# Single placing of transfers with new issue costs, a second staging place for the last weight combinations, and a section moved ahead of the first pair

## The chip, the core and the metric

The kernel runs on one core of a Trainium2 chip. The metric is device time in microseconds (us) of one execution. TensorE (PE) multiplies matrices, VectorE (DVE), ScalarE (ACT) and GpSimd (POOL) do elementwise work, and SyncE (SP) issues every transfer of this kernel, in one queue (SPq in the views). Each engine executes its instructions in the order in which the program was written out; between engines, semaphores make an instruction wait.

## The reference

Windowed attention (8 batches, 8 heads, 576 positions, head size 64, window 64), then a feed-forward layer with a squared ReLU over all 4608 tokens:

```python
scores = scale * np.matmul(q, k.transpose(0, 1, 3, 2))
mask = (rel >= 0) & (rel < 64)              # rel = query position - key position
attn = softmax(np.where(mask, scores, -1e9))
x = (attn @ v).transpose(0, 2, 1, 3).reshape(4608, 512)
out = np.maximum(x @ w_in, 0.0) ** 2 @ w_out      # w_in 512 x 2048, w_out 2048 x 512, 64-bit floats
```

## The kernel before

**Tiles.** The 4608 tokens are 12 tiles of 384. The attention of one tile is three sections (section i belongs to tile i // 3). A section has scores on TensorE (S, L233), copying and masking (o, s), a negative row maximum (z, y), exponentials on ScalarE (e, f, L261), sums and reciprocals, a product on POOL (m, L270), transposes on TensorE (X, L274), their masked copy `pt` (x, L278), the values on TensorE (V, L296) and the copies of the result into the tile's x (H, Q; L311, L313). `burst(i, j)` puts the scores of section i and the values of section j on TensorE one behind the other; `cross(i)` puts the transposes.

**Inputs of sections.** `load_qk(b, g)` loads a pair of heads of q and k into one of two halves of `raw`, by 8 transfers (L146); a transpose on VectorE (`turn`, L165) brings it into place. `load_v(b, t)` loads 128 positions of v, by 4 transfers (2 for the last t), L155; a batch's v comes in three parts of 8, 4 and 6 transfers, placed behind the softmax of three sections.

**Feed-forward.** Every matrix is held as a high and a low part, and three products make one. Tiles 0 to 3 are plain: for each of the 16 blocks f of the hidden layer, a first product (12 matmuls, `mm1`, L402), ReLU on ScalarE (`evac`, L411), square on VectorE (L416), the split (L419, L421), and a second product two steps later (9 matmuls, `mm2`, L444). Tiles 4 to 11 go in four pairs by a scheme of seven products in place of eight: `operands(j)` makes sums and differences of the pair's x and splits them (L848, L859, L860), `product(s, n)` is one of the seven products of step s (six matmuls, L896), its results are added up on VectorE (L910) and squared, and `second` (L977, L985) multiplies with w_out. A pair has eight steps s.

**Weight combinations.** The seven products need, beside blocks of w_in itself, sums of blocks. They are made once, during tiles 2 and 3, by `mixing(h)` for h = 0 to 15: six POOL operations (L530, L534) into a scratch `scr`, a cast on ScalarE (C, L536) and a subtraction on VectorE (E, L538) into `mx`, and a store of 512 KB to `mixed` in HBM (F, L540). Scratch and `mx` lie in one of two staging places, the two halves of `wide` (tile `a` in the trace); h below 12 alternates between them, and 12 to 15 all take place 0. The halves of `wide` hold the x of tiles 5 and 6 afterwards, which section 15 and section 18 begin to write. In the same time `keep` stores the split weights to `kept` (L517, 1 MB each). `wi_fetch` (L716, 256 KB) and `wo_fetch` (L724, 512 KB) bring blocks back from `mixed` and `kept` into 13 and 8 slots.

**Order.** Tiles 0 and 1 and the first two steps of tile 2 are written out by hand in a string. Everything behind is listed as operations of a `Plan` with an engine, a cost in us, what each reads and writes, and `lands`, the latency behind it. `in_order` keeps the order of TensorE as listed and simulates the other engines: each takes, of the operations that are ready, the one with the earliest due time (`late`, worked back from TensorE's times). What comes out is a fixed order for each engine. `HOP` (0.12) is added between operations and `SPARE` (1.5) before an operation of SP that waits for an engine other than TensorE. `freed(name)` lets an operation wait until the weight block whose memory the named slab will take has been read for the last time; `SLOTS` says which block that is.

In the pairs, `marks` says at which place a section's bursts and crosses stand: key 2s is ahead of the products of step s, key 2s + 1 is behind them. Section 19 (the second section of tile 6) has key 2: scores of 19 and values of 18 ahead of step 1, its transposes behind step 1.

Of the kernel before, what the change touches and what calls it, by code (L numbers as in the profile page):

```python
# [15 lines left out]
P = 128  # L16
# [13 lines left out]
def window_attention_relu2_ffn(ctx: ExitStack, tc: tile.TileContext, q, k, v, w_in, w_out, out):  # L30
# [108 lines left out]
    def load_qk(b, g):  # L139
        raw = raws[b, g] = raw_t[:, g % 2]  # L140
        for hd in range(2):
            for e in range(2):
                r = slice(32 * (2 * hd + e), 32 * (2 * hd + e) + 32)
                for n, x in enumerate((q, k)):
                    y = x[b, 4 * (g % 2) + 2 * (g // 2) + hd].rearrange("(t i) (e l) -> e i t l", i=32, e=2)[e]
                    sp.dma_start(raw[r, n].rearrange("i (t l) -> i t l", l=32), y)  # L146
# [3 lines left out]
    def load_v(b, t):  # L150
        vt = vts[b, t] = vt_t[:, t]
        for n in range(min(2, NB - 2 * t)):
            s0 = (2 * t + n) * QB
            for m in range(2):
                sp.dma_start(vt[m * QB:(m + 1) * QB, n],  # L155
                             v[b, m * H // 2:(m + 1) * H // 2, s0:s0 + QB, :].rearrange("h s d -> s h d"))
# [363 lines left out]
    def mix(op, h, which=None):  # L520
        p, kk = divmod(h, 2)
        flat = wide()[:, h % 2 if h < LAST_ODD else 0].rearrange("p a b c -> p (a b c)")
# [55 lines left out]
    for g in range(2):  # L578
# [3 lines left out]
    SLOTS = dict(t=0, xb0=1, xb1=2, xb2=3, wi0=4, wi1=5, part0=6, part1=7, hi=8, lo=9, gb0=10, gb1=11,  # L582
                 wo0=12, wo1=13, wo2=14, wo3=15)
# [51 lines left out]
    class Plan:  # L635
# [3 lines left out]
        def __call__(self, engine, cost, do, reads=(), writes=(), lands=0.0, after=()):  # L639
# [10 lines left out]
            self.ops.append((engine, cost, do, before - {n, None}, lands))  # L650

        def in_order(self):
# [10 lines left out]
            for n in reversed(range(len(ops))):  # L663
                if ops[n][0] != "pe":
                    late[n] = min([late[m] for m in after[n]], default=clock) - ops[n][1] - ops[n][4] - HOP
# [8 lines left out]
            out, at_pe = [], 0  # L674
            while len(out) < len(ops):
# [12 lines left out]
                engine, cost, _, _, lands = ops[n]  # L688
                ready[engine].remove(n)
                at_pe += engine == "pe"  # L690
                free[engine] = start + cost
                out.append(n)
                for m in after[n]:
                    missing[m] -= 1
                    hop = SPARE if ops[m][0] == "sp" and engine != "pe" else HOP
                    soon[m] = max(soon[m], start + cost + lands + hop)
# [14 lines left out]
    def wi_fetch(name, source, keys=()):  # L711
# [4 lines left out]
        plan("sp", 0.1, lambda: sp.dma_start(wi_slot(slot).bitcast(F32), source), keys, [("wi", slot)], 4.5,  # L716
             freed(wi_home(slot)[0]) if n < NWI else [])

    def wo_fetch(name, f, tick):
# [4 lines left out]
        plan("sp", 0.1, lambda: sp.dma_start(wo_slot(slot).bitcast(F32), kept[f, :, 1]), tick, [("wo", slot)], 6.0,  # L724
             freed(f"wo{slot // 2}") if n < NWO else [])
# [17 lines left out]
    def values(i):  # L743
        if SPT * 3 <= i < SPT * NTILE:
            plan("pe", 0.95, by(section, "V", i), ["pt"] + [("vt", t) for t in range(5)], ["v_ps0", "v_ps1"])

    def weigh(i):
# [65 lines left out]
    def plain2(n):  # L813
# [3 lines left out]
        for tb in range(NTB) if ends else [None]:  # L817
# [5 lines left out]
            if ends:  # L823
                to = ("part", tb) if t == 3 else ("x", tb)
                plan("act", 0.62, by(put, "Z", t, tb), [("bank", tb + 1)], [to], 0, freed("part0") if t == 3 else [])
                plan("sp", 0.1, by(put, "W", t, tb), [to], [], 3.0)
# [13 lines left out]
    def operands(j):  # L840
# [104 lines left out]
    def second(k, x):  # L945
# [40 lines left out]
        if group == 3:  # L986
            row = (NPLAIN + 2 * j) * TT + tb * P
            plan("sp", 0.1, lambda: sp.dma_start(out[row:row + P, :], parts(tb)), [kp], [], 3.0)
# [6 lines left out]
    for h in range(NMIX, 2 * NP):  # L995
        mixing(h)
    for n in range(2 * NF + LAG, NPLAIN * NF):
# [4 lines left out]
        plain2(n - LAG)  # L1002
        plain_g(n)
# [68 lines left out]
```

## Time and profile before

| | before |
|---|---|
| median of 3 runs | 860.4 us (858.29 to 1754.12) |
| the profiled execution | 860.38 us, span of its instructions 858.5 us |
| TensorE busy | 832.6 us, 97% of the span |
| VectorE, ScalarE, POOL busy | 593.2, 408.7, 185.2 us |
| chain that ended last | TensorE 88%, DMA 5%, SP's queue 4% |
| packets of the transfers | 273,011, of them 190,496 under 512 B |

The profile is one execution on the chip. All times in the views count from the start of the span. Matmuls overlap, so a stretch of TensorE is best read from the start of one group to the start of the next.

### The profile page before, as it was taken

To read this page: it belongs to the slowest core of one execution; us is meant where nothing else is said; L and a number is where in the kernel's file an instruction comes from. 1 tells how busy PE (TensorE), PEld (TensorE's weight loads), DVE (VectorE), ACT (ScalarE), POOL (GpSimd) and SP (SyncE) were. 2 spreads that over 40 slices of the span, in tenths; PEclk is the share of its full clock that TensorE was granted. 3 is DMA by queue.
4 is the path that set the end of the run, shared out by engine and by line. 5 is a ranking of instruction groups with operands and counts; after the bars stand their busy time and mean duration, and the time that the engine had idled before them with its cause. 6 is when DMAs were issued, how large, how long until landed. Compare 5 with 4: busy or idle time off the path is not lost.

```text
span 858.5 us, 17703 instructions
## 1 busy us (share of the span) xinstructions
PE 832.6 (97%) x6754; PEld 763.1 (89%) x6754; DVE 593.2 (69%) x889; ACT 408.7 (48%) x1127; POOL 185.2 (22%) x239
## 2 busy tenths in 40 slices
PE   6799999999988999999999999999999999999998
PEld 5688999899977999899999999999999999999997
DVE  5899995747764766767678766688765668545553
ACT  5787874646444644554453455344355424223221
POOL 1210003207854300112131112131111231111010
PEclk9999999999998999999999999999999999999999
DMA  9989947475786783988997788979874755776421
GB/s 221 226 260 345 338 193 139 83 169 161 184 214 218 166 161 67 288 256 182 204 282 239 212 173 205 279 173 278 254 238 129 228 185 151 264 244 212 134 76 73
DMA packets 273011, 173.92 MB, mean 203 GB/s; under 512 B 190496, under 2 KB 239648, under 8 KB 270880
## 3 DMA queue, kind: packets, MB, share of 16 engines
q1 hardware_dynamic: 272928, 172.80, 72.8%
q8 instruction: 53, 0.87, 0.4%
q14 instruction: 30, 0.25, 0.1%
HBM read 138.15 MB, written 34.60 MB: 201 GB/s over the span
## 4 chain that ended last, share of the span: by engine, by line
PE 88%; DMA 5%; SPq 4%; ACT 2%; DVE 1%; issue 1%; POOL 0%; ACTq 0%; POOLq 0%; DVEq 0%
PE banks L977 29%; PE banks L896 25%; PE banks L402 13%; PE banks L444 13%; PE banks L296 3%; PE banks L233 3%; DMA mixed<-a 2%; PE banks L274 1%; SPq L155 1%; SPq L183 1%; DMA vt<-in_v_dram 1%; ACT sel L261 1%; DMA w<-in_k_dram 1%; DMA w<-kept 1%; SPq L146 1%
## 5 line engine op out<-in xcount | busy, mean ns | idle before, releaser
L977 PE MATMUL banks<-w 128*128 128x512 f32 x1152 | 257.5, 380 | 0.0
L977 PEld LDWEIGHTS banks<-w 128*128 128x128 f32 x1152 | 215.7, 189 | 28.4
L402 PE MATMUL banks<-x,w 128*128 128x384 f32 x768 | 139.4, 332 | 8.6 <-ACT r L411 8.2
L402 PEld LDWEIGHTS banks<-x,w 128*128 128x128 f32 x768 | 128.2, 191 | 14.0 <-ACT r L411 11.3
L444 PE MATMUL banks<-w,g 128*128 128x512 f32 x576 | 136.2, 382 | 0.0
L896 PE MATMUL banks<-x,w 128*128 128x384 f32 x768 | 130.0, 326 | 0.0
L922 POOL TENSOR_TENSOR g<-g 128x384 f32<-128x384 f32 x64 | 59.5, 934 | 319.3 <-ACT g L933 282.6
L896 PEld LDWEIGHTS banks<-x,w 128*128 128x128 f32 x768 | 125.6, 189 | 0.0
L444 PEld LDWEIGHTS banks<-w,g 128*128 128x128 f32 x576 | 106.3, 189 | 14.3 <-DVE g L421 1.1
L261 ACT ACTIVATE sel<-sel,nm 128x64 f32<-128x64 f32 x272 | 90.8, 336 | 21.3 <-DVE nm L255 18.4
L896 PE MATMUL banks<-w 128*128 128x384 f32 x576 | 100.7, 329 | 0.0
L985 DVE TENSOR_TENSOR w<-w,banks 128x512 f32<-128x512 f32 x72 | 49.4, 687 | 69.9 <-PE banks L977 69.9
L896 PEld LDWEIGHTS banks<-w 128*128 128x128 f32 x576 | 93.8, 189 | 2.0
L967 ACT CAST w<-w 128x512 fp32r<-128x512 f32 x48 | 29.8, 620 | 72.9 <-PE banks L977 72.9
L411 ACT ACTIVATE r<-banks 128x384 f32<-128x384 f32 x64 | 31.5, 492 | 59.6 <-PE banks L402 59.1
L270 POOL TENSOR_TENSOR sel<-sel,nm 128x512 f32<-128x512 f32 x33 | 36.4, 1104 | 106.9 <-ACT g L933 57.9
L967 ACT CAST w<-g 128x512 fp32r<-128x512 f32 x48 | 29.6, 620 | 62.3 <-PE banks L977 58.3
L530 POOL TENSOR_TENSOR a<-w 128x256 f32<-128x256 f32 x32 | 25.9, 822 | 121.5 <-DVE w L132 79.5
L261 ACT ACTIVATION_READ_ACCUMULATOR sel<-sel,nm 128x1 f32 x272 | 51.3, 189 | 0.0
L421 DVE TENSOR_TENSOR g<-r,g 128x384 fp32r<-128x384 f32 x64 | 38.5, 601 | 18.3 <-ACT g L419 13.0
L910 DVE TENSOR_TENSOR w<-banks,r 128x384 f32<-128x384 f32 x64 | 38.3, 598 | 13.2 <-PE banks L896 12.9
L915 DVE SCALAR_TENSOR_TENSOR w<-w 128x384 f32<-128x384 f32 x64 | 46.1, 720 | 1.7
(99 smaller groups left out, 986.4 us busy)
## 6 DMA issues: line engine op xcount, KB each, us to landing
w<-mixed SPq DMA_DIRECT2D x128, 256.0 KB, 5.2
w<-kept SPq DMA_DIRECT2D x64, 512.0 KB, 6.7
w<-kept SPq DMA_DIRECT2D x96, 256.0 KB, 5.7
kept<-w SPq DMA_DIRECT2D x16, 1024.0 KB, 7.9
vt<-in_v_dram SPq DMA_DIRECT2D x144, 64.0 KB, 3.7
w<-in_moe_w_in_dram SPq DMA_DIRECT2D x16, 512.0 KB, 6.5
w<-in_moe_w_out_dram SPq DMA_DIRECT2D x16, 512.0 KB, 8.0
mixed<-a SPq DMA_DIRECT2D x16, 512.0 KB, 3.9
```

The source lines that it names most:

```text
L261: act.activation(sels[i][:, w, hd], sels[i][:, w, hd], AF.Exp, bias=nms[i][:, n], scale=SCALE, accum_out=sums[i][:, n])
L270: (dve if eng == "d" else pool).tensor_tensor(p, p, rs[i][:, :, None].broadcast_to([P, SW * 2, QB]), ALU.mult)
L402: pe.matmul(h_ps, lhsT=weights(kk, part), rhs=in_turn(x[xx][:, kk // 2, kk % 2]), start=n == 0, stop=n == 3 * NK - 1)
L421: dve.tensor_tensor(gs[n][1], rg.pop(n), gs[n][0].bitcast(F32), ALU.subtract)
L444: pe.matmul(acc(t, tb), lhsT=gg[:, ts], rhs=in_turn(weights(part)), start=f == 0 and n == 0, stop=f == NF - 1 and n == 2)
L896: pe.matmul(ps[:, :TT], lhsT=w[:, part, kk * P:(kk + 1) * P], rhs=in_turn(x[:, xx, kk]), start=n < 4 and m == 0, stop=m == 5, skip_group_c ...
L910: plan("dve", 0.6, lambda: dve.tensor_tensor(to(), ps, other(), ALU.add), [kps, ko], keys, 0, after)
L915: plan("dve", 0.57, lambda: dve.scalar_tensor_tensor(x(), x(), 0.0, x(), ALU.max, ALU.mult), [], keys)
L922: plan("pool", 0.95, lambda: pool.tensor_tensor(x(), x(), x(), ALU.mult), [], keys)
L967: plan("act", 0.62, lambda: act.copy(high(c), src()), g_keys, [kh], 0, freed("hi") if new else [])
L977: pe.matmul(ps, lhsT=gg[:, m // 2, m % 2], rhs=in_turn(wo_slot(w[m])[:, part]), start=m == 0 and n == 0, stop=m == 3 and n == 2)
L985: plan("dve", 0.72, lambda: dve.tensor_tensor(by_half(parts(tb)), by_half(parts(tb)), ordered(ps), ALU.add), [key], [kp])
```

## The change

Transfers of q, k and v in the planned part become plan operations of their own, one for each issue; in the plan, issues get costs of 0.4 to 0.6 us, and a new number `moves` for the time that a transfer holds the DMA engines, which the planner adds up one behind the other. The operations of a combination get 1.0 us of latency each. Combinations 13 and 15 use the slab t as a third place and are listed behind the first second product of tile 3. The table of slots gets another order. The scores of 19 and values of 18 move ahead of step 0, the transposes of 19 behind product 4 of step 1.

```diff
-    def load_qk(b, g):
+    def load_qk(b, g, which=range(8)):
...
-                    sp.dma_start(raw[r, n].rearrange("i (t l) -> i t l", l=32), y)
+                    if 4 * hd + 2 * e + n in which:
+                        sp.dma_start(raw[r, n].rearrange("i (t l) -> i t l", l=32), y)
...
-    def load_v(b, t):
+    def load_v(b, t, which=None):
...
+                if not which or (n, m) in which:
...
-        flat = wide()[:, h % 2 if h < LAST_ODD else 0].rearrange("p a b c -> p (a b c)")
+        if h > LAST_ODD and h % 2:
+            flat = slab("t", F32)
+        else:
+            flat = wide()[:, h % 2].rearrange("p a b c -> p (a b c)")
...
-    SLOTS = dict(t=0, xb0=1, xb1=2, xb2=3, wi0=4, wi1=5, part0=6, part1=7, hi=8, lo=9, gb0=10, gb1=11,
-                 wo0=12, wo1=13, wo2=14, wo3=15)
+    SLOTS = dict(t=0, xb0=1, xb1=2, xb2=3, wi0=4, wi1=5, hi=6, lo=7, part0=8, part1=9, wo0=10, gb0=11,
+                 wo1=12, gb1=13, wo2=14, wo3=15)
...
-                    late[n] = min([late[m] for m in after[n]], default=clock) - ops[n][1] - ops[n][4] - HOP
+                    late[n] = min([late[m] for m in after[n]], default=clock) - sum(ops[n][m] for m in (1, 4, 5)) - HOP
...
+                done = start + cost + lands
+                if moves:
+                    moved = max(moved, start + cost) + moves
+                    done = moved + lands
...
-                    soon[m] = max(soon[m], start + cost + lands + hop)
+                    soon[m] = max(soon[m], done + hop)
...
-        plan("sp", 0.1, lambda: sp.dma_start(wi_slot(slot).bitcast(F32), source), keys, [("wi", slot)], 4.5,
-             freed(wi_home(slot)[0]) if n < NWI else [])
+        plan("sp", 0.45, lambda: sp.dma_start(wi_slot(slot).bitcast(F32), source), keys, [("wi", slot)], 3.5,
+             freed(wi_home(slot)[0]) if n < NWI else [], 0.7)
...
-                    plan("sp", 0.4, by(load_v, b, t), [], [("vt", t)], 3.0)
+                    for n in range(min(2, NB - 2 * t)):
+                        for m in range(2):
+                            plan("sp", 0.6, by(load_v, b, t, [(n, m)]), [], [("vt", t, n, m)], 2.5, (), 0.3)
...
-                    plan("dve", 1.4, by(turn, b, g), [("raw", g % 2)], [("qk", g // 2, g % 2)])
+                    plan("dve", 1.4, by(turn, b, g), [("raw", g % 2, n) for n in range(8)],
+                         [("qk", g // 2, g % 2)])
...
-                    plan("sp", 0.8, by(load_qk, b, g), [], [("raw", g % 2)], 3.0)
+                    for n in range(8):
+                        plan("sp", 0.54, by(load_qk, b, g, [n]), [], [("raw", g % 2, n)], 2.5, (), 0.4)
...
-        side = h % 2 if h < LAST_ODD else 0
+        side = h % 2 if h < LAST_ODD else h % 2 * 2
         w, scr, mx = [("w", h // 2 * 2), ("w", h // 2 * 2 + 1)], ("scr", side), ("mix", side)
+        free = freed("t") if side == 2 else []
         for c in range(6):
-            plan("pool", 0.77 if c < 2 else 0.5, by(mix, "A", h, [c]), w if c < 2 else [], [scr])
-        plan("act", 0.6, by(mix, "C", h), [scr], [mx])
-        plan("dve", 0.7, by(mix, "E", h, dve), [scr], [mx])
-        plan("sp", 0.1, by(mix, "F", h), [mx], [("mixed", h // 2, h % 2)], 5.0)
+            plan("pool", 0.77 if c < 2 else 0.5, by(mix, "A", h, [c]), w if c < 2 else [], [scr],
+                 1.0 if c == 5 else 0.0, free)
+        plan("act", 0.6, by(mix, "C", h), [scr], [mx], 1.0, free)
+        plan("dve", 0.7, by(mix, "E", h, dve), [scr], [mx], 1.0)
+        plan("sp", 0.55, by(mix, "F", h), [mx], [("mixed", h // 2, h % 2)], 4.5, (), 1.4)
...
-                 a[1] + c[1], to[1], 0, freed("t") if first and to in t else [])
+                 a[1] + c[1], to[1], 0, freed("t") + [("scr", 2), ("mix", 2)] if first and to in t else [])
...
     for h in range(NMIX, 2 * NP):
-        mixing(h)
+        if h < LAST_ODD or h % 2 == 0:
+            mixing(h)
...
         plain2(n - LAG)
+        if n - LAG == 3 * NF:
+            for h in range(LAST_ODD + 1, 2 * NP, 2):
+                mixing(h)
...
-            marks.setdefault(16 * j + (2 * r if r else -4), []).append(by(burst, i, i - 1))
-            marks.setdefault(16 * j + (2 * r if r else -4) + 1, []).append(by(cross, i))
+            m = 16 * j + (2 * r if r else -4)
+            m, n = (0, (1, 4)) if m == 2 else (m, m + 1)
+            marks.setdefault(m, []).append(by(burst, i, i - 1))
+            marks.setdefault(n, []).append(by(cross, i))
...
                 product(s, n)
+                for mark in marks.get((s, n), []):
+                    mark()
```

The other costs: `wo_fetch` 0.1 with landing 6.0 becomes 0.4, 3.5 and `moves` 1.4; `keep` 0.1 and 8.0 becomes 0.6, 3.5 and 2.8; the stores of the output 0.1 and 3.0 become 0.4, 3.0 and 0.7. `values` reads the v pieces by their new keys.

## Rows read from the trace of the kernel before

**Rows 1.** TensorE's waits from 184 us to the end: total, times, longest

```profile
PE banks L402 <- ACT r L411: 6.8, 3, 2.8
PE banks L296 <- DMA vt<-in_v_dram: 1.0, 1, 1.0
```

**Rows 2.** timeline of TensorE, undisturbed steps: start, us, instructions, idle before

```profile
222.51 1.10 PE L233 MATMUL banks<-qk 64*64 64x128 f32 x32
...
224.43 2.21 PE L444 MATMUL banks<-w,g 128*128 128x512 f32 x9
226.48 2.11 PE L402 MATMUL banks<-x,w 128*128 128x384 f32 x12
228.43 2.11 PE L444 MATMUL banks<-w,g 128*128 128x512 f32 x9
```

**Rows 3.** timeline of TensorE where it waited for L411

```profile
241.57 2.21 PE L444 MATMUL banks<-w,g 128*128 128x512 f32 x9
246.22 2.22 PE L402 MATMUL banks<-x,w 128*128 128x384 f32 x12 [2.44 <-ACT r L411]
...
252.16 2.11 PE L444 MATMUL banks<-w,g 128*128 128x512 f32 x9
255.79 2.22 PE L402 MATMUL banks<-x,w 128*128 128x384 f32 x12 [1.52 <-ACT r L411]
...
264.21 2.10 PE L444 MATMUL banks<-w,g 128*128 128x512 f32 x9
269.14 4.21 PE L402 MATMUL banks<-x,w 128*128 128x384 f32 x12 [2.83 <-ACT r L411]
273.28 1.99 PE L233 MATMUL banks<-qk 64*64 64x128 f32 x32
...
276.00 2.21 PE L444 MATMUL banks<-w,g 128*128 128x512 f32 x9
```

**Rows 4.** windows: busy of each engine, granted clock, DMA share, GB/s

```profile
269.00:272.00 3.00, 2.86 (x9) 2.86 (x10) 1.71 (x4) 1.93 (x5) 2.84 (x5) 0.50 0.76 252
```

**Rows 5.** timeline of TensorE where it waited for v

```profile
358.21 1.10 PE L233 MATMUL banks<-qk 64*64 64x128 f32 x32
...
361.08 1.20 PE L296 MATMUL banks<-pt,vt 64*64 64x128 f32 x32 [1.00 <-DMA vt<-in_v_dram]
362.20 3.19 PE L896 MATMUL banks<-w 128*128 128x384 f32 x18
```

**Rows 6.** timeline of ScalarE, two casts of combinations

```profile
243.35 0.62 ACT L536 CAST a<-a 128x512 fp32r<-128x512 f32 x1 [6.01 <-DMA mixed<-a]
...
265.43 0.62 ACT L536 CAST a<-a 128x512 fp32r<-128x512 f32 x1 [4.88 <-DMA mixed<-a]
```

**Rows 7.** timeline of VectorE, two subtractions of combinations

```profile
229.35 0.64 DVE L538 TENSOR_TENSOR a<-a 128x512 fp32r<-128x512 f32 x1
...
252.48 0.68 DVE L538 TENSOR_TENSOR a<-a 128x512 fp32r<-128x512 f32 x1
```

**Rows 8.** timeline of SP's queue; first and last of 16 raw loads

```profile
229.09 0.61 SPq L146 DMA_DIRECT2D raw<-in_q_dram  x1
...
239.03 0.50 SPq L146 DMA_DIRECT2D raw<-in_k_dram  x1
239.62 1.28 SPq L540 DMA_DIRECT2D mixed<-a  x2
...
259.76 0.52 SPq L540 DMA_DIRECT2D mixed<-a  x1
...
352.13 3.77 SPq L155 DMA_DIRECT2D vt<-in_v_dram  x4
```

**Rows 9.** line L540, the stores to mixed

```profile
DMA to landing us min/median/max: 3.5/3.9/6.6
```

**Rows 10.** timeline of VectorE, first subtraction of the operands

```profile
324.84 0.96 DVE L848 TENSOR_TENSOR w<-a,x 128x768 f32<-128x768 f32 x1
```

**Rows 11.** waits of SP's queue: total, times, longest

```profile
SPq L716 <- PE banks L896: 154.8, 97, 10.9
```

More of the change, by code (lines that the diff above doesn't have):

```diff
@@ L154, in load_v @@
             for m in range(2):
-                sp.dma_start(vt[m * QB:(m + 1) * QB, n],
-                             v[b, m * H // 2:(m + 1) * H // 2, s0:s0 + QB, :].rearrange("h s d -> s h d"))
+                if not which or (n, m) in which:
+                    sp.dma_start(vt[m * QB:(m + 1) * QB, n],
+                                 v[b, m * H // 2:(m + 1) * H // 2, s0:s0 + QB, :].rearrange("h s d -> s h d"))
     def get_turned(b, d):
@@ L637, in __init__, with __call__ @@
             self.ops, self.wrote, self.read = [], {}, {}
-        def __call__(self, engine, cost, do, reads=(), writes=(), lands=0.0, after=()):
+        def __call__(self, engine, cost, do, reads=(), writes=(), lands=0.0, after=(), moves=0.0):
             n = len(self.ops)
@@ L649, in __call__ @@
                 self.wrote[key], self.read[key] = n, set()
-            self.ops.append((engine, cost, do, before - {n, None}, lands))
+            self.ops.append((engine, cost, do, before - {n, None}, lands, moves))
         def in_order(self):
@@ L673, in in_order @@
                     ready[op[0]].append(n)
-            out, at_pe = [], 0
+            out, at_pe, moved = [], 0, 0.0
             while len(out) < len(ops):
@@ L687, in in_order @@
                 start, n = best
-                engine, cost, _, _, lands = ops[n]
+                engine, cost, _, _, lands, moves = ops[n]
                 ready[engine].remove(n)
@@ L723, in wo_fetch @@
         wo[name] = slot
-        plan("sp", 0.1, lambda: sp.dma_start(wo_slot(slot).bitcast(F32), kept[f, :, 1]), tick, [("wo", slot)], 6.0,
-             freed(f"wo{slot // 2}") if n < NWO else [])
+        plan("sp", 0.4, lambda: sp.dma_start(wo_slot(slot).bitcast(F32), kept[f, :, 1]), tick, [("wo", slot)], 3.5,
+             freed(f"wo{slot // 2}") if n < NWO else [], 1.4)
     def block(f, half):
@@ L744, in values @@
         if SPT * 3 <= i < SPT * NTILE:
-            plan("pe", 0.95, by(section, "V", i), ["pt"] + [("vt", t) for t in range(5)], ["v_ps0", "v_ps1"])
+            plan("pe", 0.95, by(section, "V", i), ["pt"] + [("vt", t, n, m) for t in range(5) for n in range(2) for m in range(2)],
+                 ["v_ps0", "v_ps1"])
     def weigh(i):
@@ L825, in plain2 @@
                 plan("act", 0.62, by(put, "Z", t, tb), [("bank", tb + 1)], [to], 0, freed("part0") if t == 3 else [])
-                plan("sp", 0.1, by(put, "W", t, tb), [to], [], 3.0)
+                plan("sp", 0.4, by(put, "W", t, tb), [to], [], 3.0, (), 0.7)
     def mixing(h):
-        side = h % 2 if h < LAST_ODD else 0
+        side = h % 2 if h < LAST_ODD else h % 2 * 2
         w, scr, mx = [("w", h // 2 * 2), ("w", h // 2 * 2 + 1)], ("scr", side), ("mix", side)
+        free = freed("t") if side == 2 else []
         for c in range(6):
-            plan("pool", 0.77 if c < 2 else 0.5, by(mix, "A", h, [c]), w if c < 2 else [], [scr])
-        plan("act", 0.6, by(mix, "C", h), [scr], [mx])
-        plan("dve", 0.7, by(mix, "E", h, dve), [scr], [mx])
-        plan("sp", 0.1, by(mix, "F", h), [mx], [("mixed", h // 2, h % 2)], 5.0)
+            plan("pool", 0.77 if c < 2 else 0.5, by(mix, "A", h, [c]), w if c < 2 else [], [scr],
[3 more added lines that the diff above has]
+        plan("sp", 0.55, by(mix, "F", h), [mx], [("mixed", h // 2, h % 2)], 4.5, (), 1.4)
     def operands(j):
@@ L987, in second @@
             row = (NPLAIN + 2 * j) * TT + tb * P
-            plan("sp", 0.1, lambda: sp.dma_start(out[row:row + P, :], parts(tb)), [kp], [], 3.0)
+            plan("sp", 0.4, lambda: sp.dma_start(out[row:row + P, :], parts(tb)), [kp], [], 3.0, (), 0.7)
     starts = {2: (10, 9), 5: (11, 10), 9: (12, 11), 13: (13, 0), 16: (14, 12), 18: (15, 13), 21: (16, 14), 23: (17, 15),
@@ L1006, in window_attention_relu2_ffn @@
         if m % 3 == 0 and 10 <= 9 + m // 3 < NF:
-            plan("sp", 0.1, by(keep, 9 + m // 3), [("w", 9 + m // 3), ("tick", n)], [], 8.0)
+            plan("sp", 0.6, by(keep, 9 + m // 3), [("w", 9 + m // 3), ("tick", n)], [], 3.5, (), 2.8)
     for n in range(NPLAIN * NF - LAG, NPLAIN * NF):
```

## Prediction

> **What bounds the kernel.** I read the windows of the stages first, then TensorE's waits, TensorE's timeline at each wait, and last, for the engine named there, what it waited for in its turn. The waits of TensorE from 184 us on, which is about where the written-out order ends and the planner's order begins, come down to two kinds: 6.8 us in three waits for ScalarE's evacuation of the first product (L411), and 1.0 us in one wait for a load of v [rows 1]. Everything else after 184 us is TensorE going from product to product, so the most that a better order can give is what these stretches cost. What they cost is more than their idle time, and the reader should take it from starts.
>
> Undisturbed, a section's scores and values take 224.43 − 222.51 = 1.92 us, the second product after them 2.05, the next first product 1.95 [rows 2]. Against that [rows 3]: 241.57 to 246.22 is 4.65 where 2.05 is normal (2.60 lost); 252.16 to 255.79 is 3.63 (1.68 lost, against 1.95); 264.21 to 269.14 is 4.93 (2.98 lost). The first product at 269.14 then takes 4.14 instead of 1.95 (2.19 lost), and scores and values from 273.28 to 276.00 take 2.72 instead of 1.92 (0.80 lost): the granted clock stands at 0.50, the 1.2 GHz level, after the idle stretch before it [rows 4]. Together 10.25 us. The fourth place: scores at 358.21 to the next product at 362.20 take 3.99 instead of 1.92, so 2.07 us, with the wait for v in the middle [rows 5].
>
> **Why these stalls stand there.** ScalarE executes in order. At 243.35 its cast of a weight combination (L536) had waited 6.01 us for a store to `mixed`, at 265.43 another 4.88 [rows 6]; the evacuation L411 is queued behind it, and TensorE behind that. The stores were late because of SP's queue and not because of their data: the subtraction that feeds the first of them begins at 229.35 and takes 0.64, so it was ready at 229.99; the one of 259.76 was ready at 252.48 + 0.68 = 253.16 [rows 7]. SP issued them at 239.62 and 259.76, 9.6 and 6.6 us later, since it was in the middle of 16 loads of raw, 229.09 to 239.03, then 16 more just so [rows 8]. One issue takes some 0.5 us there, eight take 4.3; the planner's cost for the eight is 0.8, and for the store 0.1.
>
> **The change, part by part.** *Single placing and issue times.* No instruction is added: the same 8 issues a pair of heads and 4 to 8 a part of v, now eight plan entries of 0.54 where there was one of 0.8, and 0.6 a piece where there was 0.4 for a whole tile. What changes is the order, on all engines, because the planner's clock changes. SP's queue picks by due time, so a store can go between two raw loads: it then waits for one issue, about 0.5 us, not for 16. Would that be soon enough? A store lands 3.5 to 6.6 us after its issue, the middle 3.9 [rows 9]. Issued when ready, and with the longest landing: 229.99 + 0.5 + 6.6 = 237.1, and ScalarE was free for its cast at 243.35 − 6.01 = 237.3; 253.16 + 0.5 + 6.6 = 260.3, and ScalarE was free at 265.43 − 4.88 = 260.55. So even the long end removes both waits, and the half clock with them. The bounds of this term: 0 (the order comes out alike) and 10.25; I take 10.25, since both examples end there.
>
> The transfers could be the limit instead of their order. In the kernel before, most packets are small (the table, 190,496 of 273,011 under 512 B). The Trainium skill, "DMA: Bandwidth & Descriptors", section "Specifications", says that transfers under 512 B don't reach line rate; by that alone the loads of raw would hold the stores up however they are issued, and this part would give nothing (the second rival). The trace agrees that packets are small, and speaks against the conclusion with a landing time of 6.6 us at the worst.
>
> *Longer latencies for the combinations.* The POOL steps of the next combination wait only for the subtraction; its cast waits for the store. By the plan's own costs one such round of a staging place (cast 0.6, subtraction 0.7, the spare 1.5, store and landing 5.1, hops) was some 8.1 us and is now 0.6 + 0.7 + 2 × 1.0 + 1.5 + 0.55 + 1.4 + 4.5 + hops, some 11.5. ScalarE therefore meets each cast later and finds its store landed. Six rounds on the odd place are 69 us. The values of section 15, which overwrite that place, come by the plan's costs after 22 first products and 21 second ones at 1.95, eight scores at 0.85, six values at 0.95 and six transposes at 0.38, some 98 us from the plan's start: there is room.
>
> *Second place for combinations 13 and 15.* Same 6 POOL instructions, one cast, one subtraction, one store each, in the slab t, in place of the even place of `wide`. Place 0 then carries 8 combinations (92 us), not 10, and is needed sooner by the moved section. New wait: the first subtraction of the operands (L848), at 324.84 [rows 10], must wait for both stores, and behind it on VectorE stand the squares and splits that TensorE needs. The slab comes free with the first second product of tile 3, the one at 276.00 [rows 3]; POOL's 3.5 by the plan and two rounds of cast 0.6, subtraction 0.7, issue 0.5 and landing 3.9 to 6.6 are 15 to 20 us, so they are over near 298, with some 26 us of cover (the stalls that vanish stand before both ends). I cost it at nothing; without that cover it costs what is late, at most the 5 us of one round's store.
>
> *The section ahead of the first pair.* Scores of 19 and values of 18, 1.92 us of TensorE, go seven products (7 × 0.98 = 6.9 us) forward; TensorE's sum is the same. The values of 18 read the old v, so the load of the next part of v can leave 6.9 us sooner: at 352.13 − 6.9 = 345.2, and with the measured 361.08 − 352.13 = 8.95 us until TensorE went on it is there at 354.2 [rows 5, 8]. Values of 19 want it near 359: 5 us over. The transposes of 19 also go before the last two products of their step, which ends the small wait for the probabilities. Bounds: 0 and 2.07; I take 2.07. ScalarE and VectorE get the softmax of 19 (2.8 us of exponentials) beside the first products and the last operand splits; product 0 itself starts 1.9 us later, which gives those splits room.
>
> *Slot table.* It changes only what the planner believes about when two slabs come free; two weight fetches may leave a few us sooner. Nothing.
>
> *The rest, 343 us to the end.* No wait of TensorE but the one for v is listed there, so there is nothing to gain; the order of SP is drawn anew there too, so there is something to lose (third rival).
>
> **Sum.** Profiled execution 860.38 us, which is the median (860.4) within 0.02. The 1.9 us of it that lie outside the span stay. 860.38 − 10.25 − 2.07 = 848.06. I add 0.4, an allowance of mine for small new waits: **848.5 us**.
>
> **Rivals.** (1) *One large stall stays* (chance 0.20). The casts have a fixed place in ScalarE's queue, and one bad estimate of a landing is enough. For: 16 combinations pass through four queues, between section work with due times of its own. Against: the longer latencies in the plan. Price: the third stall with its half clock, 2.98 + 2.19 + 0.80 = 5.97, so 854.0 to 854.5.
> (2) *The stores still leave or land late* (0.11): the loads of raw have the earlier due times and stay ahead, or the DMA engines are the limit. Then only the 2.07 are won: 858.3.
> (3) *Slower: SP stands before a weight fetch with v behind it* (0.07). SP waits for a product to free a weight slot 97 times, 154.8 us, up to 10.9 at once [rows 11]. A piece of v that is now placed just in time by its due time, behind such a fetch, makes the values wait as at 361.08, at 2.07 us each. Eleven parts of v are loaded after 343 us. From six that wait on, the gain of 12.3 is gone; with eight it is 848.1 + 16.6 = 864.7. Against: before, ten of the eleven came without a wait.
> The forecast itself has 0.60 (848.0 to 850.5), and 0.02 lie below.
>
> **Range.** 847.0 to 856.0 takes the forecast and rival 1 and leaves 2 in 10 out. Two per cent, about what a measurement of this kernel tells from no change, is 17.2 us: under 843.2 would need more than all the waits after 184 us, 0.02; over 877.6 would need the third rival at more than all eleven parts, 0.02; so 0.96 within.
>
> **What would show it.** Right: no wait of L402 for L411 after 184 us; casts L536 with no wait for `mixed` over 1 us; stores standing singly between raw loads in SP's queue; granted clock 1.00 from 260 to 280; values of 19 without a wait for v. Wrong: waits of values for v after 343 us (rival 3), casts waiting for stores at another place (rivals 1 and 2), L848 waiting for a store from t, or a stall at the first products because their splits come behind the softmax of 19.

## The result, and the profile after

The changed kernel takes 847.96 us, the median of 4 runs (847.21 to 848.63); the kernel before takes 859.31 us, the median of 3 (858.29 to 860.4). The ratio is 0.987, with a 95% interval of 0.985 to 0.989: some 11 us faster, a gain of 1.3%. The forecast was 848.5 us. Two executions, one of the kernel before (1754.12 us) and one of one_place below (1240.0 us), fell in a slow state of the chip and are left out of every median and ratio here.

The change shifts line numbers: L402 is now L404, L411 L413, L536 L541, L538 L543, L540 L545, L848 L864, L896 L912. The list of TensorE's waits from 186 us to the end is empty; the wait for L411 and the one for v [rows 1] are gone. TensorE's timeline after, at the places that answer to [rows 3] and [rows 5] (columns as there):

```profile
240.82 2.21 PE L446 MATMUL banks<-w,g 128*128 128x512 f32 x9
242.87 2.11 PE L404 MATMUL banks<-x,w 128*128 128x384 f32 x12
...
346.99 1.10 PE L235 MATMUL banks<-qk 64*64 64x128 f32 x32
347.91 0.96 PE L298 MATMUL banks<-pt,vt 64*64 64x128 f32 x40
348.81 3.19 PE L912 MATMUL banks<-w 128*128 128x384 f32 x18
```

The second product behind the scores of section 13 goes to the next first product in 242.87 − 240.82 = 2.05 us, where it was 4.65 before. Scores and values of section 20 and 19 take 348.81 − 346.99 = 1.82 us, where it was 3.99. The granted clock, in the window of [rows 4]:

```profile
269.00:272.00 3.00, 3.00 (x18) 2.76 (x17) 1.81 (x2) 3.00 (x18) 2.89 (x6) 1.00 0.40 90
```

It is 1.00 where it was 0.50. To see where the whole difference of the two spans (858.5 and 845.1 us) comes from, I cut each profiled execution at three starts that every variant has: the first product of the plan's first step, the three last second products of tile 3, and the first product of step 2 of the first pair (362.20 in [rows 5], 348.81 above). The work of TensorE between two cuts is the same in all variants.

| stretch | before | after | difference |
|---|---|---|---|
| start to the plan's first step | 188.43 | 187.68 | 0.75 |
| to the end of tile 3 (stretch 1) | 147.88 | 137.40 | 10.48 |
| to step 2 of the first pair (stretch 2) | 25.89 | 23.73 | 2.16 |
| to the end | 496.30 | 496.29 | 0.01 |

The head belongs to the part written out by hand, which the change doesn't touch; in the twelve variants below it lies between 188.3 and 191.3, so a single execution says less than the two stretches do. So 10.48 and 2.16 are what the change gives, and the rest of the kernel is as long as it was.

**How ScalarE got free.** In the kernel before, ScalarE had executed three evacuations, and one other cast, between the cast that ended at 226.81 and the one of [rows 6] at 243.35, for which it was free at 237.34:

```profile
229.52 0.47 ACT L411 ACTIVATE r<-banks 128x384 f32<-128x384 f32 x1
...
232.77 0.48 ACT L411 ACTIVATE r<-banks 128x384 f32<-128x384 f32 x1
...
236.85 0.49 ACT L411 ACTIVATE r<-banks 128x384 f32<-128x384 f32 x1 [1.56 <-PE banks L402]
```

These are the rows of the changed kernel's ScalarE, VectorE and SP that answer to [rows 6], [rows 7] and [rows 8]:

```profile
224.31 0.63 ACT L541 CAST a<-a 128x512 fp32r<-128x512 f32 x1
...
227.95 0.46 ACT L413 ACTIVATE r<-banks 128x384 f32<-128x384 f32 x1
...
231.77 0.49 ACT L413 ACTIVATE r<-banks 128x384 f32<-128x384 f32 x1 [1.63 <-PE banks L404]
...
236.10 0.49 ACT L413 ACTIVATE r<-banks 128x384 f32<-128x384 f32 x1 [2.65 <-PE banks L404]
...
240.00 0.49 ACT L413 ACTIVATE r<-banks 128x384 f32<-128x384 f32 x1 [2.02 <-PE banks L404]
...
241.88 0.62 ACT L541 CAST a<-a 128x512 fp32r<-128x512 f32 x1
```

```profile
227.78 0.65 DVE L543 TENSOR_TENSOR a<-a 128x512 fp32r<-128x512 f32 x1
```

```profile
225.04 0.55 SPq L147 DMA_DIRECT2D raw<-in_q_dram  x1
...
233.20 1.43 SPq L147 DMA_DIRECT2D raw<-in_k_dram  x1
234.67 2.58 SPq L157 DMA_DIRECT2D vt<-in_v_dram  x4
237.36 1.27 SPq L545 DMA_DIRECT2D mixed<-a  x2
```

The store that was ready at 227.78 + 0.65 = 228.43 is issued at 237.36, 8.9 us later, behind the last nine of 16 loads of raw in a row and four of v. That is nearly as late as before (9.6 us). What is different is ScalarE's queue: between the cast at 224.31 and the one at 241.88 it now executes four evacuations L413 and no other cast, and when it comes to the cast, the store has landed: the row has no idle time, where the cast of [rows 6] had 6.01 us. The planner did not bring the store forward; in its simulation the store leaves late, and it put the cast behind it.

Further on, single placing does show:

```profile
248.60 0.50 SPq L147 DMA_DIRECT2D raw<-in_q_dram  x1
249.20 1.24 SPq L545 DMA_DIRECT2D mixed<-a  x2
250.49 2.70 SPq L147 DMA_DIRECT2D raw<-in_k_dram  x1
```

```profile
300.04 0.56 SPq L147 DMA_DIRECT2D raw<-in_k_dram  x1
300.71 0.52 SPq L545 DMA_DIRECT2D mixed<-w  x1
301.32 3.71 SPq L545 DMA_DIRECT2D mixed<-a  x1
...
305.79 1.09 SPq L147 DMA_DIRECT2D raw<-in_q_dram  x1
```

Here stores stand between loads of raw of one pair of heads. What the second of these places may be worth, the run `grouped` below shows.

### The profile page after: what moved, and what is told of

It is laid out like the page before. It is cut to its first block, busy times and chain, and to the rows that moved or that the text cites. A ratio compares the mean times of both kernels' runs of the same rounds, so it can differ in the third digit from the quotient of the medians.

```text
span 845.1 us, 17706 instructions
## 1 busy us (share of the span) xinstructions
PE 829.0 (98%) x6754; PEld 761.2 (90%) x6754; DVE 590.5 (70%) x889; ACT 407.3 (48%) x1127; POOL 184.9 (22%) x239
## 4 chain that ended last, share of the span: by engine, by line
PE 86%; SPq 5%; DVE 3%; DMA 3%; issue 2%; ACT 1%; POOL 0%; DVEq 0%; ACTq 0%; POOLq 0%
PE banks L993 29%; PE banks L912 26%; PE banks L446 11%; PE banks L404 11%; PE banks L235 3%; PE banks L298 3%; DMA w<-in_moe_w_out_dram 2%; PE banks L276 2%; SPq L147 1%; SPq L185 1%; SPq L157 1%; DVE a L123 1%; DVE a L125 1%; SPq L104 1%; DVE g L423 1%
## 5 line engine op out<-in xcount | busy, mean ns | idle before, releaser
L404 PE MATMUL banks<-x,w 128*128 128x384 f32 x768 | 137.1, 328 | 1.9 <-ACT r L413 1.4
L404 PEld LDWEIGHTS banks<-x,w 128*128 128x128 f32 x768 | 126.6, 189 | 6.1 <-ACT r L413 3.3
L912 PE MATMUL banks<-x,w 128*128 128x384 f32 x768 | 130.3, 326 | 0.0
L912 PEld LDWEIGHTS banks<-x,w 128*128 128x128 f32 x768 | 125.6, 189 | 0.0
L912 PE MATMUL banks<-w 128*128 128x384 f32 x576 | 100.7, 329 | 0.0
L912 PEld LDWEIGHTS banks<-w 128*128 128x128 f32 x576 | 93.8, 189 | 1.9
L413 ACT ACTIVATE r<-banks 128x384 f32<-128x384 f32 x64 | 31.5, 492 | 66.8 <-PE banks L404 64.6
L280 DVE TENSOR_TENSOR pt<-banks,masks 128x1024 f32<-128x1024 f32 x33 | 40.3, 1220 | 10.9 <-PE banks L276 10.9
L926 DVE TENSOR_TENSOR w<-banks,r 128x384 f32<-128x384 f32 x64 | 38.5, 601 | 13.3 <-PE banks L912 13.0
```

The costliest lines, as they stand in the source:

```text
L280: dve.tensor_tensor(pts[i].rearrange("p (w n) q -> p w n q", n=2), ps_t[i][:, :, None, :].broadcast_to([P, SW, 2, P]), masks.rearrange("p ...
L404: pe.matmul(h_ps, lhsT=weights(kk, part), rhs=in_turn(x[xx][:, kk // 2, kk % 2]), start=n == 0, stop=n == 3 * NK - 1)
L912: pe.matmul(ps[:, :TT], lhsT=w[:, part, kk * P:(kk + 1) * P], rhs=in_turn(x[:, xx, kk]), start=n < 4 and m == 0, stop=m == 5, skip_group_c ...
L926: plan("dve", 0.6, lambda: dve.tensor_tensor(to(), ps, other(), ALU.add), [kps, ko], keys, 0, after)
```

## The experiments

All times in the table are of profiled executions, cut as above (us); median and ratio are of the runs beside the kernel before on the same chip. The variants ran on more than one chip and at several times, and the kernel before moved with them by up to 2.6 us, so a median is to be held against the one in its own line and not against that of another variant. The undisturbed lengths are 137.4 and 23.7.

| variant | stretch 1 | stretch 2 | median | before, beside it | ratio, 95% interval |
|---|---|---|---|---|---|
| before | 147.88 | 25.89 | 859.31 | | |
| changed | 137.40 | 23.73 | 847.96 | 859.31 | 0.987 (0.985 to 0.989) |
| moved_only | 144.98 | 23.73 | 856.80 | 861.87 | 0.994 (0.993 to 0.996) |
| not_moved | 137.41 | 26.32 | 854.10 | 861.87 | 0.990 (0.987 to 0.994) |
| grouped | 145.55 | 23.73 | 856.53 | 861.87 | 0.993 (0.991 to 0.995) |
| singles_old_costs | 146.81 | 26.06 | 860.29 | 861.87 | 0.998 (0.996 to 1.000) |
| latency_only | 149.59 | 25.72 | 863.34 | 860.13 | 1.004 (1.002 to 1.005) |
| costs_only | 137.56 | 26.03 | 851.52 | 860.13 | 0.991 (0.988 to 0.993) |
| no_latency | 137.40 | 23.73 | 849.80 | 860.13 | 0.988 (0.985 to 0.990) |
| one_place | 137.40 | 23.73 | 849.76 | 860.13 | 0.988 (0.984 to 0.991) |
| costs_moved | 137.59 | 23.72 | 848.53 | 859.86 | 0.987 (0.983 to 0.990) |
| singles_real_costs | 137.40 | 25.74 | 850.67 | 859.86 | 0.989 (0.985 to 0.992) |
| raw_cost_only | 137.87 | 25.80 | 853.51 | 859.86 | 0.993 (0.991 to 0.996) |
| grouped_one_place | 137.41 | 27.48 | 855.10 | 859.86 | 0.994 (0.992 to 0.996) |

Single executions of one kernel differ by up to 7.0 us (latency_only, 860.25 to 867.28), so where the medians and the stretches disagree, the stretches say what the order does, and the medians what a user gets.

**The section alone** (moved_only: the edit of `marks` on the kernel before).

```diff
-            marks.setdefault(16 * j + (2 * r if r else -4), []).append(by(burst, i, i - 1))
-            marks.setdefault(16 * j + (2 * r if r else -4) + 1, []).append(by(cross, i))
+            m = 16 * j + (2 * r if r else -4)
+            m, n = (0, (1, 4)) if m == 2 else (m, m + 1)
+            marks.setdefault(m, []).append(by(burst, i, i - 1))
+            marks.setdefault(n, []).append(by(cross, i))
```

> The kernel before with one part of the change alone: scores of 19 and values of 18 ahead of step 0, transposes of 19 behind product 4 of step 1. Theory A (the move frees the load of v, its worth stands apart from the stalls at 240 to 276 us): the first product of step 0 to the first of step 2 shrinks by 2.0 to 2.3 us, no wait of the values for v after 343 us, the three waits for L411 stay; time about 858 us. Rival B (the move only helps when the planner's costs are right too): the planner redraws all queues from its old costs and the wait for v comes back at another place; no gain, 860 us or above.

Stretch 2 is 23.73, 2.16 us less, with no wait for v: theory A. Stretch 1, which the edit doesn't touch, is 2.9 us shorter as well, since other due times give another order, with two waits for L411 in place of three:

```profile
246.78 2.88 PE L402 MATMUL banks<-x,w 128*128 128x384 f32 x12 [2.34 <-ACT r L411]
...
269.56 2.22 PE L402 MATMUL banks<-x,w 128*128 128x384 f32 x12 [2.72 <-ACT r L411]
```

**All but the section** (not_moved: the changed kernel with the old `marks`).

> The changed kernel with the section back at its old place (scores of 19 and values of 18 ahead of step 1). Theory A: about 2.0 to 2.3 us longer than the changed kernel (850 us), with a wait of the values of 19 for v. Rival B (single pieces of v with real costs are enough, the move is worth nothing by itself): the same as the changed kernel, 848 us, no wait.

Stretch 2 is 26.32 and the wait is back:

```profile
349.13 1.10 PE L235 MATMUL banks<-qk 64*64 64x128 f32 x32
350.55 0.45 PE L298 MATMUL banks<-pt,vt 64*64 64x128 f32 x8 [0.31 <-DVE pt L280]
352.12 1.49 PE L298 MATMUL banks<-pt,vt 64*64 64x128 f32 x32 [1.12 <-DMA vt<-in_v_dram]
```

Theory A again, and 2.59 us, a little more than the 2.16 that the kernel before had there. The median, 854.1, lies 4 us over what I expected, with runs from 849.61 to 856.07, on a chip where the kernel before took 861.87, 2.6 us more than beside the changed kernel; the profiled one has its other surplus in the head (189.8) and behind step 2 (497.75), where it has no wait.

**Grouped loads at real costs** (grouped: the changed kernel with these two plan entries).

```diff
-                    for n in range(8):
-                        plan("sp", 0.54, by(load_qk, b, g, [n]), [], [("raw", g % 2, n)], 2.5, (), 0.4)
+                    plan("sp", 4.32, by(load_qk, b, g), [], [("raw", g % 2, n) for n in range(8)], 2.5, (), 0.4)
...
-                            plan("sp", 0.6, by(load_v, b, t, [(n, m)]), [], [("vt", t, n, m)], 2.5, (), 0.3)
+                    plan("sp", 0.6 * len(pieces), by(load_v, b, t), [], [("vt", t, n, m) for n, m in pieces], 2.5, (), 0.3)
```

> The changed kernel, but the eight loads of raw are one plan entry of 4.32 us again and the loads of one v tile one entry of 0.6 us a piece: real issue times without single placing. Theory C (what removes the stalls is that the planner knows how late a store leaves, and puts ScalarE's cast behind its landing): no wait of L402 for L411, 848 to 849 us. Rival D (my prediction: a store must be able to go between two loads of raw): a store stands behind 8 or 16 loads again, and at least one of the three stalls comes back, 851 to 858 us.

Rival D's number: one stall of 8.15 us, at a new place. SP's queue, VectorE's subtraction, ScalarE's cast and TensorE there:

```profile
302.77 0.68 DVE L543 TENSOR_TENSOR a<-a 128x512 fp32r<-128x512 f32 x1
```

```profile
305.11 0.41 SPq L147 DMA_DIRECT2D raw<-in_q_dram  x1
...
313.80 0.52 SPq L545 DMA_DIRECT2D mixed<-w  x1
...
315.07 5.83 SPq L157 DMA_DIRECT2D vt<-in_v_dram  x8
321.02 0.55 SPq L545 DMA_DIRECT2D mixed<-a  x1
```

```profile
324.82 0.62 ACT L541 CAST a<-a 128x512 fp32r<-128x512 f32 x1 [8.41 <-DMA mixed<-a]
```

```profile
319.08 2.11 PE L446 MATMUL banks<-w,g 128*128 128x512 f32 x9
326.61 4.21 PE L404 MATMUL banks<-x,w 128*128 128x384 f32 x12 [5.42 <-ACT r L413]
```

```profile
327.00:330.00 3.00, 3.00 (x11) 3.00 (x11) 2.57 (x5) 0.80 (x2) 0.00 (x0) 0.50 0.33 50
```

The subtraction is ready at 303.45, the store leaves at 321.02, behind three fetches, eight loads of raw, another store, a fetch and eight loads of v; the cast waits 8.41 us, TensorE 5.42, and the clock falls to 1.2 GHz. The eight loads of raw alone took 8.6 us here, from 305.11 to 313.69, twice the 4.32 that the plan has for them. In the changed kernel the store of the same combination was ready at 296.16 and leaves at 301.32, between two loads of raw. So this edit costs 8 us here, and nothing at the three old stalls, which are gone in this variant too. The 8 us are not shown to be single placing alone: `moves` is booked once for a group, 0.4 us for eight loads of raw where eight single entries book 3.2, so the planner's picture of the DMA engines changed with the grouping.

**Single loads at old costs** (singles_old_costs: on the kernel before; each of the 8 loads of raw and each piece of v an entry of its own, at 0.1).

```diff
-                    plan("sp", 0.8, by(load_qk, b, g), [], [("raw", g % 2)], 3.0)
+                    for n in range(8):
+                        plan("sp", 0.1, by(load_qk, b, g, [n]), [], [("raw", g % 2, n)], 3.0)
```

> The kernel before with the loads of raw and v placed singly, at the old costs of 0.1 us an issue, nothing else changed. Theory C: the planner still takes SP to be nearly free, the loads still stand ahead of the stores and the casts still come too early; the three stalls stay, 857 to 861 us. Rival D (single placing does it): the stalls go, 850 to 852 us (the wait for v after 343 us may stay).

(The loads of v get 0.1 a piece in the same way.) Theory C: stretch 1 is 146.81, 1.07 us less than before, and the casts wait as before:

```profile
246.40 0.62 ACT L538 CAST a<-a 128x512 fp32r<-128x512 f32 x1 [6.17 <-DMA mixed<-a]
...
268.47 0.62 ACT L538 CAST a<-a 128x512 fp32r<-128x512 f32 x1 [4.87 <-DMA mixed<-a]
```

Single entries alone would let a store pass; at 242.68 it still left behind 16 loads of raw, and in the plan SP looks nearly free.

**Latencies alone, costs alone** (latency_only and costs_only, both on the kernel before).

```diff
-            plan("pool", 0.77 if c < 2 else 0.5, by(mix, "A", h, [c]), w if c < 2 else [], [scr])
-        plan("act", 0.6, by(mix, "C", h), [scr], [mx])
-        plan("dve", 0.7, by(mix, "E", h, dve), [scr], [mx])
+            plan("pool", 0.77 if c < 2 else 0.5, by(mix, "A", h, [c]), w if c < 2 else [], [scr],
+                 1.0 if c == 5 else 0.0)
+        plan("act", 0.6, by(mix, "C", h), [scr], [mx], 1.0)
+        plan("dve", 0.7, by(mix, "E", h, dve), [scr], [mx], 1.0)
```

```diff
-                    plan("sp", 0.4, by(load_v, b, t), [], [("vt", t)], 3.0)
+                    plan("sp", 0.6 * 2 * min(2, NB - 2 * t), by(load_v, b, t), [], [("vt", t)], 2.5)
-                    plan("sp", 0.8, by(load_qk, b, g), [], [("raw", g % 2)], 3.0)
+                    plan("sp", 4.32, by(load_qk, b, g), [], [("raw", g % 2)], 2.5)
```

> The kernel before with only the latencies of 1.0 us for the last POOL step, the cast and the subtraction of a combination; issue costs as before. Theory C1 (the issue costs of the loads carry the gain): casts still meet stores that stand behind 16 loads, at least 6 of the 10 us stay, 855 to 860 us. Rival C2 (any later placing of the casts is enough): no wait for L411, 850 us.

> The kernel before with only the issue costs of the grouped loads changed (8 loads of raw 4.32 us, v 0.6 us a piece), no single placing, no latencies, no third place, no moved section. Theory C1: most of the 10.25 us go, 849 to 852 us with the wait for v still there. Rival C2 (the latencies carry it): the stalls stay in part, 855 to 859 us.

Theory C1 both times. With the latencies alone stretch 1 is 149.59, longer than before, and the median is 863.3, over the 855 to 860 that I expected. With the costs of two plan entries changed (their landing went from 3.0 to 2.5 with them), and the loads still in groups, it is 137.56: 10.32 of the 10.48 us. SP's queue there is nearly that of the kernel before, and ScalarE's is not:

```profile
230.13 0.65 DVE L538 TENSOR_TENSOR a<-a 128x512 fp32r<-128x512 f32 x1
```

```profile
227.24 0.55 SPq L146 DMA_DIRECT2D raw<-in_q_dram  x1
...
235.87 0.50 SPq L146 DMA_DIRECT2D raw<-in_k_dram  x1
236.41 2.93 SPq L155 DMA_DIRECT2D vt<-in_v_dram  x4
239.44 1.28 SPq L540 DMA_DIRECT2D mixed<-a  x2
```

```profile
226.50 1.15 ACT L536 CAST a<-a 128x512 fp32r<-128x512 f32 x2
...
230.30 0.47 ACT L411 ACTIVATE r<-banks 128x384 f32<-128x384 f32 x1
...
233.97 0.49 ACT L411 ACTIVATE r<-banks 128x384 f32<-128x384 f32 x1 [1.47 <-PE banks L402]
...
238.30 0.49 ACT L411 ACTIVATE r<-banks 128x384 f32<-128x384 f32 x1 [2.24 <-PE banks L402]
...
242.19 0.49 ACT L411 ACTIVATE r<-banks 128x384 f32<-128x384 f32 x1 [2.26 <-PE banks L402]
...
244.08 0.62 ACT L536 CAST a<-a 128x512 fp32r<-128x512 f32 x1
```

Ready at 230.78, issued at 239.44, 8.7 us late; and four evacuations stand between the casts, as in the changed kernel. Casts still wait for stores in this variant, 8.1 us in four waits, the longest 3.9, and TensorE waits for none of them. So the planner need not put every cast behind the landing of its store; waits of up to 3.9 us were covered where these casts now stand.

**Without the latencies, without the third place** (no_latency and one_place, both on the changed kernel; the first has 0.0 for the three 1.0; the second this).

```diff
-        if h > LAST_ODD and h % 2:
-            flat = slab("t", F32)
-        else:
-            flat = wide()[:, h % 2].rearrange("p a b c -> p (a b c)")
+        flat = wide()[:, h % 2 if h < LAST_ODD else 0].rearrange("p a b c -> p (a b c)")
...
-        side = h % 2 if h < LAST_ODD else h % 2 * 2
+        side = h % 2 if h < LAST_ODD else 0
...
-        if h < LAST_ODD or h % 2 == 0:
-            mixing(h)
+        mixing(h)
...
-        if n - LAG == 3 * NF:
-            for h in range(LAST_ODD + 1, 2 * NP, 2):
-                mixing(h)
```

> The changed kernel without the three latencies of 1.0 us. Theory C1: the landing estimate of the store is enough, 848 to 849 us, waits of casts under 1 us. Rival C2: casts wait for stores again by up to 3 us and a wait for L411 comes back, 850 to 854 us.

> The changed kernel with combinations 12 to 15 all on staging place 0, listed at the start as before; all else as changed. Theory E (the third place is there so that section 18 finds its place free in time): place 0 carries 10 combinations, in the plan 10 x 11.5 = 115 us of the 140 that it has, so nothing waits: 848 to 849 us. Rival F (the third place carries part of the gain): the copy of section 18 waits for a store, a stall of 2 to 6 us near 331 us, 850 to 854 us.

Both stretches are at their undisturbed length in both variants: neither part is needed. The casts do wait for stores, 2.3 us in two waits and 3.9 us in two (the longest 1.7 and 2.5, over the 1 us that I expected without the latencies), and TensorE doesn't. The medians, both 849.8, are 2 us over the changed kernel's, in other runs; the profiles have that in the head (190.8 and 190.1) and not in what was edited.

**Two edits** (costs_moved: the diffs of costs_only and moved_only together, on the kernel before).

> The kernel before with two edits alone: the real issue costs of the grouped loads (8 loads of raw 4.32 us, v 0.6 us a piece) and the section ahead of the first pair. Theory G (these two carry the whole gain): the first planned product to the end of tile 3 takes 137.4 to 137.6 us, the first pair's start 23.7, so 848 to 849 us. Rival H (whether a group stands ahead of a store is chance, and every redrawing of the queues can bring a stall): a stall for L411 of 3 to 8 us somewhere from 240 to 330 us, 851 to 857 us.

Theory G: 137.59 and 23.72, and 848.5 us, the changed kernel's time with two costs and one moved section. The whole rest of the change, single placing included, adds nothing to these two stretches. Behind step 2 this variant is 1.2 us longer (497.50 us), with a wait of TensorE of 0.9 us at 391.64, for VectorE's adding up of the products (L910), that the changed kernel doesn't have; which part of the rest takes it away isn't shown.

**Single loads at real costs, and one cost** (singles_real_costs: as singles_old_costs with 0.54 and 0.6; raw_cost_only: only the 4.32; the landing goes from 3.0 to 2.5 in both).

> The kernel before with the loads of raw and v placed singly at 0.54 and 0.6 us an issue; no section moved, no latencies, no third place, other costs old. Theory G (real costs, grouped or single): the first planned product to the end of tile 3 takes 137.4 to 137.6 us, the wait for v stays, 850 to 851 us. Rival (the grouping or its absence matters): another number for that stretch, 140 us or more.

> The kernel before with one cost changed: the group of 8 loads of raw 4.32 us instead of 0.8. Theory G1 (the three stalls stood behind 16 loads of raw, so this one number removes them): the stretch to the end of tile 3 at most 138 us, 850 to 851 us. Rival (the loads of v, 8 issues of 0.6 each, matter as well): one of the stalls stays, 853 to 857 us.

The first has 137.40 in stretch 1, the second 137.87, with one wait for L411 of 0.2 us left; the wait for v stays in both, as it must. The plan entry of the raw group carried 10.0 of the 10.48 us; its cost went from 0.8 to 4.32, and that its landing of 2.5 does it instead wasn't tried apart. The second's median, 853.5, is over the 851 that I expected, its runs lie between 850.55 and 857.09, and its profile is of a run of 850.71, so what the longer runs have more is not seen.

**Grouped loads, one place** (grouped_one_place: the edits of grouped and one_place together).

> The changed kernel with the loads of raw and v grouped (real costs) and combinations 12 to 15 all on place 0. Theory J (grouping costs where the late listing of 13 and 15 pushes the last stores to 300 us and later, in front of the loads that section 18 needs): without the third place no stall, 848 to 849 us. Rival H (grouping costs by itself): the stall of some 8 us at 321 us or another one stays, 853 to 857 us.

The time is rival H's, and theory J, no stall, failed. Stretch 1 is 137.41, so the stall at 321 us needs the third place's late listing, or what else it moves; but stretch 2 is 27.48, with a stall of another kind (ScalarE's L538 and SP's L542 are the cast and the store here):

```profile
338.94 1.38 SPq L542 DMA_DIRECT2D mixed<-a  x1
```

```profile
348.11 0.59 ACT L313 COPY a<-banks 128x512 f32<-128x512 f32 x1 [2.31 <-DMA mixed<-a]
```

```profile
348.84 0.63 PE L276 MATMUL banks<-ident,sel 128*128 128x128 f32 x4 [3.56 <-ACT a L313]
```

The last store of place 0 leaves at 338.94 and the copy of section 18, which goes into that place, waits for it until 348.11; TensorE waits 3.56. This is rival F's mechanism, which one_place had not shown. There the last store of place 0 leaves 10.6 us after the start of tile 3's last second products (338.12 − 327.48) and the copy doesn't wait; here it leaves 13.3 us after it (338.94 − 325.69) and lands after 9.2 us, where no store of one_place took over 6.6. The profiled execution, of 851.6 us, is the shortest of eight, with 855.1 as the median; what the longer ones have more is not seen.

## Why the prediction was right, point by point

**The sum.** I had 10.25 for the three stalls with their half clock; they measured 10.48. I had 2.07 for the section; it measured 2.16. The end from step 2 on, where I saw nothing to gain, moved by 0.01. The allowance of 0.4 for new waits wasn't used. Taking the losses from starts and not from idle times is what made the sum: the idle times of [rows 1] are 7.8, and would have given 852.6. That the first term came out at its upper bound is in part luck, since the step that was to bring it there failed.

**The mechanism of the first part was half right.** That ScalarE's cast waits for a store, that the store stands behind the loads of raw, and that this is TensorE's wait, is shown by costs_only and raw_cost_only, which change nothing but what the planner believes of the loads and end the stalls. How the change's order does it is another matter: the step that failed is "a store can go between two raw loads: it then waits for one issue, about 0.5 us, not for 16". At the place of the first stall the store still left 8.9 us late, behind 16 loads, where I had 0.5 us. The casts were placed later in ScalarE's queue instead. My other sentence, "ScalarE therefore meets each cast later and finds its store landed", was the right one for the changed kernel, where no cast waits, but I gave it to the latencies of 1.0 us, and those do nothing (no_latency) or harm (latency_only); it is the issue costs that move the casts. That every cast finds its store landed isn't needed either, as the 8.1 us of such waits in costs_only show.

**What single placing is for.** Not for the old stalls: singles_old_costs won 1 us of 10 and costs_only all but 0.16 without it. With the changed kernel's other costs, grouping loses 8.15 us beside the third place (grouped) and 3.75 us without it (grouped_one_place, stretch 2), in both with the smaller booking of `moves`, which wasn't tried apart; with the other costs of the kernel before, grouped loads lose nothing in these stretches (costs_moved).

**The third place: nothing,** as I had it (one_place); L864, the subtraction of [rows 10], starts at 313.62 with no wait, and the last store from the slab t left at 300.71. But the cover was not the 26 us that I counted: that store took 6.5 us to land, at 307.2, so 6.4 us were left, and the two rounds took 40 us from POOL's first step at 267.06, where I had 15 to 20. In grouped the store left at 313.80, and the subtraction did wait for it, 2.0 us. With grouped loads it only puts a stall of 8.15 in the place of one of 3.75. The slot table by itself wasn't tried.

**The section.** The pieces of v left from 331.53 on, and values of 19 at 347.91 found them landed. I had moved the load by 6.9 us and counted 5 us over. Its worth is the same in moved_only and not_moved, within half a us.

**The rivals.** Rival 1, a stall that stays, didn't happen in the changed kernel, and did in grouped, at another place and of 8.15 where I had 6.0. Rival 2, the transfers as the limit, falls: from 240 to 280 us the DMA engines were busier after than before (0.90 to 0.80 of their time) without a stall, and the longest landing of a store was 7.4 us against 6.6. Rival 3, pieces of v behind a waiting fetch, would show as waits of the values for v after 343 us; there is none, though SP still waits 144.7 us in 91 waits for weight slots.

What stays open: why the head of the kernel and single executions differ by several us without any edit there; and which of the edits of the third place makes the stall at 321 us in grouped, its later stores or the order that comes of them, and whether the smaller booking of `moves` has a part in it.

## What to carry to other kernels

Where a planner writes out the order of in-order engines, an issue cost that is five times too small on one queue shows up as a stall of another engine: look at what the waiting instruction waits for, and then at what stood ahead of that in its own queue. Correct the planner's cost from the measured issue time first; it took the costs of two entries here to win ten of twelve us, and splitting entries, latency margins and a further buffer won nothing more in the two stretches beside them and the moved section. The worth of such parts has to be tested one by one. Price a stall from the start of one step to the start of the next, since restarts and the granted clock add to the idle time.

## What I had not expected of the hardware

The clock's fall after an idle stretch isn't a matter of its length alone: in the kernel before, 2.83 us idle at 266 us were followed by the 1.2 GHz level, with 2.19 us lost on the next first product [rows 3]; in moved_only 2.72 us at nearly the same place were followed by a first product of normal length (2.22), and 2.34 us at 244 us by one of 2.88. TensorE's groups of instructions in the 8.4 us ahead of the first two of these idle stretches are the same, so the work just before doesn't tell them apart either.

Two other runs show it more sharply. In latency_only 1.88 us idle were followed by a first product of 3.42 us, during which the granted clock fell to 0.50, the 1.2 GHz level; in grouped_one_place 3.56 us idle (ahead of 348.84, shown above) were followed by a granted clock of 1.00 (timeline of the first, then the windows of each, columns as in [rows 4]):

```profile
330.76 3.42 PE L402 MATMUL banks<-x,w 128*128 128x384 f32 x12 [1.88 <-ACT r L411]
```

```profile
332.00:334.00 2.00, 2.00 (x8) 2.00 (x8) 1.49 (x3) 0.00 (x0) 0.00 (x0) 0.50 0.00 0
```

```profile
348.80:350.00 1.20, 1.16 (x9) 1.19 (x10) 0.42 (x1) 0.00 (x0) 0.00 (x0) 1.00 1.03 354
```

What decides it, these runs don't show. For an estimate, a stall should be priced with the clock's fall and without it.

Moving a section by 7 products changed stalls 60 us and more ahead of it, by 2.9 us (moved_only): with a planner of this kind no edit is local, and the cuts between common starts are what tells an edit's own worth from what it stirs.
